# The last down projection of a two-layer FNet/GLU kernel as seven products, with weight combinations made on chip

## The chip, the cores and the metric

The kernel runs on one core of a Trainium2 chip. A core has five engines with a queue of their own each: TensorE (PE, with its weight loads shown apart as PEld), VectorE (DVE), ScalarE (ACT), GpSimd (POOL) and SyncE (SP), which here only issues DMA transfers. Each engine takes its instructions strictly in order and waits where one needs the result of another engine. The metric is the time of one execution in device microseconds; the median of three runs is given.

## The reference

Two layers of the same form; `x` is 2048 x 640, and `B_w_gate` and `B_w_up` are 640 x 1728, `B_w_down` 1728 x 640.

```python
def _A_ref(x, dft_seq_re, dft_seq_im, dft_hid_re, dft_hid_im):
    a = jnp.einsum("bsd,ed->bse", x, dft_hid_re)
    b = jnp.einsum("bsd,ed->bse", x, dft_hid_im)
    return jnp.einsum("ts,bse->bte", dft_seq_re, a) - jnp.einsum("ts,bse->bte", dft_seq_im, b)

def _B_ref(x, w_gate, w_up, w_down):
    g = jnp.einsum("bsd,df->bsf", x, w_gate)
    u = jnp.einsum("bsd,df->bsf", x, w_up)
    return jnp.einsum("bsf,fd->bsd", _sigmoid(g) * u, w_down)

for layer in range(2):
    x = x + _A_ref(_layernorm(x), ...)
    x = x + _B_ref(_layernorm(x), ...)
```

All data are float32. The kernel gets float32 accuracy from float16 matmuls: each operand is split in a high and a low part (high = cast on ACT, low = the rest, made on DVE), and a product is three matmuls, high x high, high x low and low x high (`PASSES`).

## The kernel before

`x` stays on chip as 16 tiles of 128 rows (`X`). The Fourier sublayer uses the symmetries of the matrices, so it tests on the way that the matrices given have them: `test_rows`, `test_cols`, `test_hidden_rows` and `test_hidden_cols` load pieces into two spare rooms by DMA, DVE folds them, ACT squares and sums (`square_rest`, L1337), and `test_all` reduces everything to one flag at the end. If the flag were set, a second, general program would run. Maxima of the weights (`test_w`, `test_gu`, L232) belong to these tests.

The GLU sublayer goes by four blocks of 512 rows (`b` = 0 to 3; the prediction calls layer 2's blocks 1 to 4). Each block has a gate/up stage and a down stage.

**Gate/up.** The hidden width 1728 is 13 tiles of 128 (`j` = 0 to 12) and one tile of 64 (`j` = 13). Most blocks compute two tiles per step by `seven`: gate and up of two half blocks of rows form a 2 x 2 scheme which takes seven products in place of eight (`part_one` to `part_seven`, matmuls at L1151, 128 x 256). A product is added up in a PSUM bank, copied out in between by ACT (`snap`, L1155), and DVE joins the copies (L1187, L1188). In the step behind, ACT takes the sigmoid (`gate`, L1197), DVE multiplies (`up`, L1207 and L1209), and `up_parts` splits the result into high and low (L1218 on ACT, L1219 on DVE) as the tile `ht` of the hidden activations. A step of two tiles is 108 matmuls (the first 90).

**Down.** For each of four row tiles `i`, 13 x 3 + 2 matmuls for each of two halves of the 640 columns (L1304, 128 x 320; the 64-row tile needs two). Then DVE adds the bank to `X` (L1319), and in layer 2 the row tile is stored (`store_x`). Tiles of the mirrored rows (`GB`, `GC`; `i` = 1 and 2) are stored by an indirect DMA of POOL (L381), the others by SP (L385).

**Order.** `steps` is the list of PE's stages. `at(u, f)` puts a job beside step `u`; a block of gate/up has 14 step numbers and the down behind it 8 (two for each row tile), so a step number of the third down is `block[3] - 8` to `block[3] - 1`. In `seven`, `some(n)` emits the jobs of the n-th quarter of a step between the products. Whatever is emitted earlier stands earlier in its engine's queue.

**Places.** On-chip memory is cut into units of 512 B per partition. 170 of them (units 218 to 387) are handed out by `Slots.take`, mostly to the place that has been free longest; a load into a place waits for the last reader of what lay there. For each tile of gate/up, `load_s` brings the high and low parts of the gate weight (`G`, 5 units), the four sums (`S`, 8 units) and the up weight (`U`, 3 units, or 5 for the maxima) back from DRAM, on SP. In layer 2's last block all of `U` comes in, because `test_gu` takes the maxima of `G` and `U` there. Fixed places hold `X` (80 units), two transposed inputs `XW` (34 each, by turns) and the split down weights (70).

Lines of the profile that the prediction's steps touch: `row_stats` L418, `pair_apply` L501, `pair_parts` L519 and L520, `pair_transpose` L526 (DMA transposes of the next block's input), `load_s` L1068 to L1074, `split` L239 and L241, `test_cols` L1376 to L1379 (and `test_rows` L1359 to L1362), `load_hidden_rows` L1413, `load_hidden_cols` L1422, `test_hidden_cols` L1426 and L1427.

Of the kernel before, what the change touches and what calls it, by code (L numbers as in the profile page):

```python
# [16 lines left out]
P = 128  # L17
# [32 lines left out]
DS = 2.0**11  # L50
# [4 lines left out]
PH = 2.0**-16  # L55
# [13 lines left out]
NT = 17  # L69
XTU = NT * 2  # L70
# [4 lines left out]
class Slots:  # L75
# [5 lines left out]
    def __init__(self, big):  # L81
        self.big = big
        self.live = {}
        self.freed = {}
        self.clock = 0
        self.close = False

    def take(self, n, high):
        taken = sorted(self.live.values())
        if self.close:  # L90
# [9 lines left out]
            else:  # L100
                a = min((a for f in free for a in {f[0], f[1] - n}),
# [17 lines left out]
    def new(self, a, n):  # L119
        s = Slot(self.big[:, a * UNIT : (a + n) * UNIT], (a, a + n))  # L120
        self.live[id(s)] = s.span
        return s
# [78 lines left out]
def folded(ctx, tc, pool, dram, big, acc, flag, x, ct, wh, wg, wu, wc, wd, out):  # L201
# [66 lines left out]
    def take(n, *key, high=False):  # L268
        key = key if len(key) > 1 else key[0]
        assert key not in held, key  # L270
        held[key] = slots.take(n, high)
# [105 lines left out]
    def store_x(i, g, c):  # L377
# [10 lines left out]
        for p, n in ((1, 15), (16, P - 16)):  # L388
            nc.sync.dma_start(by_twos(out, s + 2 * p, n, c), v[p : p + n])

# [141 lines left out]
    def first_combine(i):  # L532
# [11 lines left out]
    def first_parts(i):  # L544
# [6 lines left out]
    def first_transpose(i):  # L551
# [171 lines left out]
    def spill(i):  # L723

        for key in "eo":
            keep(take_parts(key, i)[:, :, :, :EC], key, i)
            drop(key, i)

# [338 lines left out]
    def load_s(j, whole=False):  # L1067
        nc.sync.dma_start(take(5, "G", j).f16, kept["w", 0, j])  # L1068
        if ("S", j) not in held:
            nc.sync.dma_start(take(8, "S", j).f16, kept["s", j])  # L1070
        if whole:
            nc.sync.dma_start(take(5, "U", j).f16, kept["w", 1, j])
            return
        nc.sync.dma_start(take(3, "U", j).f16.rearrange("p (q c) -> p q c", q=2),  # L1074
                          kept["w", 1, j].rearrange("p (q c) -> p q c", q=2)[:, :, 256:])
# [50 lines left out]
    def gated_parts(j):  # L1126
# [30 lines left out]
    def part_one(b, j):  # L1157
# [3 lines left out]
        v, w = (take(4, n, j, high=6).f32 for n in ("hv", "hw"))  # L1161
# [41 lines left out]
    def up(j):  # L1203
# [7 lines left out]
        drop("U", j)  # L1211

    def up_parts(j):
        if j not in late:
            return
        late.remove(j)
        v, s = held["hv", j].f32, take(4, "ht", j, high=True)
# [4 lines left out]
    def seven(b, j):  # L1222
# [20 lines left out]
        def mm(some):  # L1243
            ps, k = bank() if last else (None, None)
            for i in js:
                part_one(b, i)
# [15 lines left out]
            up_parts(earlier[0])  # L1262
# [7 lines left out]
            up_parts(earlier[1])  # L1270
# [4 lines left out]
            for i in js:  # L1275
                part_three(b, i)
            if last:
# [3 lines left out]
                up_parts(j)  # L1281
# [3 lines left out]
    def gate_tail(s, ps):  # L1285
# [6 lines left out]
        drop("hf", NF)  # L1292

    def down(b, i, j0, j1, store, es=(0, 1)):
# [18 lines left out]
        def post():  # L1313
# [7 lines left out]
            if store:  # L1321
                store_x(b, i, slice(es[0] * EH, (es[-1] + 1) * EH))
# [559 lines left out]
```

## Time and profile before

| | us |
|---|---|
| median of three runs | 1155.17 |
| lowest and highest | 1154.68, 1155.48 |
| the profiled execution | 1155.22 |
| its span, first to last instruction | 1153.3 |
| layer 2: down 1, gate/up 2 | 44.5, 82.7 |
| down 2, gate/up 3 | 44.5, 80.6 |
| down 3, gate/up 4 | 44.5, 80.8 |
| down 4, from there to the end | 44.6, 6.4 |

The span is that of the profiled execution, and the 1.9 us between its two numbers lie around it. A row of a group of instructions gives the line, engine, operation and tile shapes, then the busy time of the group in us and the mean of one in ns, then the time that the engine stood idle before them and what ended it. Of matmuls the mean is longer than the distance from one to the next, since they overlap: the pace is busy time by count. In a row of the timeline the first number is the start in the span, the second the length. A row of the waits gives the total, the times and the longest. The DMA share is the mean busy share of the core's 16 DMA engines.

### The profile page before, as it was taken

Reading aid. Unit: us, or ns where it says so; the run is one execution under the profiler, and the core shown is the slowest. Engines: PE = TensorE matmul, PEld = TensorE weight load, DVE = VectorE, ACT = ScalarE, POOL = GpSimd, SP = SyncE. Lnnn points to the kernel's source line nnn. Section 1 sums busy time; section 2 is a strip of 40 time slices with the busy share of each in tenths; the row PEclk is TensorE's granted clock in tenths of the full one; section 3 lists DMA queues with packets and bytes.
Section 4 is the critical chain, followed back from the end, with each engine's and each line's share of the span. In section 5 each row is a group of like instructions: output and inputs, shape, how many; then the busy total and the mean of one; then the engine's idle time right before and its main releaser. Section 6 shows DMA issues by size and latency. Waiting matters only on the chain.

```text
span 1153.3 us, 23284 instructions
## 1 busy us (share of the span) xinstructions
PE 1121.5 (97%) x9000; PEld 880.4 (76%) x9000; DVE 750.8 (65%) x1673; ACT 522.4 (45%) x1132; POOL 362.1 (31%) x581
## 2 busy tenths in 40 slices
PE   6699999999999999999999999999999999999997
PEld 2467446788878887888776888778887888788875
DVE  7996878668747676576547667726874457526740
ACT  6864485255525653365424446314551455225420
POOL 2312645232545454421530035022363112221000
PEclk9999999999999999999999999999999999999999
DMA  8418676985495949888412386566659851897401
GB/s 275 141 45 258 222 272 204 267 265 186 153 274 165 252 159 220 243 233 263 142 56 90 95 235 215 125 219 212 195 165 242 298 171 66 177 254 205 143 19 38
DMA packets 160758, 215.04 MB, mean 186 GB/s; under 512 B 74690, under 2 KB 107355, under 8 KB 160638
## 3 DMA queue, kind: packets, MB, share of 16 engines
q1 hardware_dynamic: 142078, 165.53, 48.5%
q0 software_dynamic: 18560, 47.93, 13.7%
q8 instruction: 72, 1.18, 0.4%
q14 instruction: 48, 0.39, 0.1%
HBM read 172.99 MB, written 25.81 MB: 172 GB/s over the span
## 4 chain that ended last, share of the span: by engine, by line
PE 82%; DVE 3%; DMA 2%; issue 1%; ACT 1%; SPq 0%; POOL 0%; DVEq 0%; ACTq 0%
PE acc L1151 41%; PE acc L1304 31%; PE acc L1104 4%; PE acc L899 2%; PE acc L1240 2%; PE acc L817 1%; DMA big<-in_ct 1%; DVE big L241 1%; DMA kept_w<-big 0%; DMA big<-in_wu 0%; DVE big L1188 0%; PE acc L1235 0%; SPq L257 0%; ACT big L1337 0%; DVE big L971 0%
## 5 line engine op out<-in xcount | busy, mean ns | idle before, releaser
L1151 PE MATMUL acc<-big 128*128 128x256 f16 x4698 | 516.5, 273 | 1.9 <-ACT big L1155 1.9
L1151 PEld LDWEIGHTS <-big 128*128 128x128 f16 x4698 | 459.7, 98 | 56.4 <-issue 2.3
L1304 PE MATMUL acc<-big 128*128 128x320 f16 x2624 | 357.7, 299 | 0.0
L1304 PEld LDWEIGHTS <-big 128*128 128x128 f16 x2624 | 256.8, 98 | 99.4
L1353 POOL DMA_DIRECT2D big<-in_ct x256 | 174.7, 688 | 220.4 <-DVE big L1362 122.0
L1155 ACT ACTIVATE big<-acc 128x256 f32<-128x256 f32 x348 | 129.5, 381 | 250.7 <-PE acc L1151 249.5
L1219 DVE TENSOR_TENSOR big<-big 128x512 f16<-128x512 f32 x87 | 60.0, 689 | 107.3 <-ACT big L1218 107.3
L1337 ACT ACTIVATE big<-big 128x768 f32<-128x768 f32 (+8 forms) x104 | 79.5, 764 | 106.6 <-DVE big L1362 65.0
L1104 PE MATMUL acc<-big 128*128 128x256 f16 (+1 forms) x705 | 114.9, 325 | 0.6 <-DVE big L241 0.4
L1104 PEld LDWEIGHTS <-big 128*128 128x128 f16 x705 | 68.5, 98 | 46.0 <-DVE big L241 2.0
L1319 DVE SCALAR_TENSOR_TENSOR big<-acc,big 128x320 f32<-128x320 f32 x64 | 28.5, 485 | 102.4 <-PE acc L1304 102.4
L1197 ACT ACTIVATE big<-big 128x512 f32<-128x512 f32 x87 | 53.5, 627 | 43.6 <-DVE big L1188 43.0
L241 DVE SCALAR_TENSOR_TENSOR big<-big 128x640 f16<-128x640 f32 (+6 forms) x81 | 62.4, 805 | 12.1 <-ACT big L239 12.1
L1370 POOL DMA_DIRECT2D big<-in_ct x40 | 27.4, 686 | 114.6 <-ACT big L1337 66.7
L1207 DVE SCALAR_TENSOR_TENSOR big<-acc,big 128x256 f32<-128x256 f32 x87 | 36.4, 418 | 38.7 <-PE acc L1151 33.5
L1188 DVE TENSOR_TENSOR big<-big,acc 128x512 f32<-128x512 f32 x87 | 59.2, 681 | 3.5 <-PE acc L1151 3.3
L239 ACT ACTIVATE big<-big 128x640 f16<-128x640 f32 (+7 forms) x81 | 50.5, 666 | 23.6 <-POOL big L1044 12.9
L1218 ACT ACTIVATE big<-big 128x512 f16<-128x512 f32 x87 | 54.4, 625 | 8.6 <-DVE big L1209 7.7
L899 PE MATMUL acc<-big 128*128 128x321 f16 (+3 forms) x324 | 49.0, 300 | 1.1 <-DVE big L241 1.1
L1187 DVE TENSOR_TENSOR big<-big 128x256 f32<-128x256 f32 x87 | 36.4, 418 | 14.2 <-ACT big L1155 14.1
L519 ACT ACTIVATE big<-big 128x384 f16<-128x384 f32 (+2 forms) x48 | 28.9, 648 | 35.9 <-DVE big L501 14.9
L899 PEld LDWEIGHTS <-big 128*128 128x128 f16 (+3 forms) x324 | 28.2, 95 | 20.3 <-issue 7.7
(194 smaller groups left out, 1033.2 us busy)
## 6 DMA issues: line engine op xcount, KB each, us to landing
big<-kept_s SPq DMA_DIRECT2D x84, 512.0 KB
big<-kept_w SPq DMA_DIRECT2D x115, 320.0 KB
big<-in_ct POOLq DMA_DIRECT2D x256, 128.0 KB, 4.0
big<-kept_w SPq DMA_DIRECT2D x74, 192.0 KB
kept_w<-big SPq DMA_DIRECT2D x27, 320.0 KB
big<-in_ct POOLq DMA_DIRECT2D x32, 256.0 KB, 5.1
kept_s<-big SPq DMA_DIRECT2D x13, 512.0 KB
big<-in_wg SPq DMA_DIRECT2D x18, 320.0 KB
```

Of the source, the lines that this page charges most:

```text
L241: nc.vector.scalar_tensor_tensor(dl, src, s, dh, op0=OP.mult, op1=OP.subtract)
L899: nc.tensor.matmul(ps[:m, :EC], z[:, at : at + m], w[:, 384 * wp : 384 * wp + EC], start=(d == 0 and zp == HI and wp == HI), stop=(d == ND ...
L1104: nc.tensor.matmul(ps, w[wp][:, d * P : (d + 1) * P], xt[:, xp, :], start=(d == 0 and wp == HI and xp == HI), stop=(d == ND - 1 and wp == LO))
L1151: nc.tensor.matmul(ps, wt, xt, start=start and n == 0, stop=n == len(todo) - 1, skip_group_check=not start)
L1155: nc.scalar.activation(dst, ps, AF.Copy)
L1188: nc.vector.tensor_tensor(v, v, other, op=OP.add)
L1197: nc.scalar.activation(v, v, AF.Sigmoid, scale=SG)
L1218: nc.scalar.activation(s.parts[HI], v, AF.Copy)
L1219: nc.vector.tensor_tensor(s.parts[LO], v, s.parts[HI], op=OP.subtract)
L1304: nc.tensor.matmul(held["pd", e][0][:, :EH], held["ht", j].parts[hp][:, i * P : (i + 1) * P], held["w", 2, j].parts[wp][:, e * EH : (e + 1 ...
L1337: nc.scalar.activation(v, v, AF.Square, accum_out=new_sum()[:p])
L1353: nc.gpsimd.dma_start(v[:, g], bass.AP(ct.tensor, (r * S + row) * S, [[P, NS], [d * S, 16], [1, P]]))
```

## The change

In layer 2's last block (`PAIRED = (), (3,)`) the down is made of pairs of hidden tiles, `NP = 6` pairs for `j` = 0 to 11: rows of the block in two halves, a pair's two tiles, and the two column halves form a 2 x 2 times 2 x 2 product, which takes seven products. Tiles 12 and 13 are added in the plain way.

- `up_parts` calls `first_parts` and `second_parts`, and `sum_parts` follows at the end of the step: they make, split and keep three of the four quarters (`A`, 6 units a pair) and four sums of them (`AS`, 8 units a pair).
- The right sides' combinations are made in the third down: `load_raw` (POOL) loads raw weight tiles, `make_t` forms four differences in place on DVE, `split_t` splits them into `TT`, which lies over `X`'s tiles 0 to 7 and over the `XW` that is free then.
- `down_pairs` runs the seven products, adds them up in four banks for each of two row tiles, and adds to `X` also in the middle of a sum.
- Stores of row tiles of the first three blocks are put beside the gate/up behind (`store_later`).
- `test_gu` goes to layer 2's third block, with the whole `U` loaded there, and the last block loads the part of `U`. In it `G` and `U` share a place of 8 units, and the three loads are put at different times.
- Tests of hidden rows and columns are put later and closer together; hidden columns are loaded by POOL. In layer 1 one row (`fw`) is kept in DRAM for a while. The sums that end the Fourier sublayer for the third block (`combine`, `join_hidden`, `add_hidden` with `q` = 2) are put 3.2 steps earlier in both layers, so that two of them lie in the first gate/up and not in the first down; the load of a block's second tile is put 1.3 steps later.
- `DS` and `PH`, powers of two, change from 2^11 and 2^-16 to 2^9 and 2^-18.

```diff
+NP = 6
+PAIRED = (), (3,)
...
-    def take(self, n, high):
+    def take(self, n, high, top=0):
         taken = sorted(self.live.values())
+        if top:
+            free = [a for a in [top - n * (i + 1) for i in range(NP)] + list(range(UNITS - n, FIX - 1, -2))
+                    if all(a + n <= c or d <= a for c, d in taken)]
+            assert free, f"no room for {n}: {taken}"
+            return self.new(free[0], n)
+        if self.fours and not high:
+
+            m = -n % 4 + n
+            free = [a for a in range(-FIX % 4 + FIX, UNITS - m + 1, 4) if all(a + m <= c or d <= a for c, d in taken)]
+            assert free, f"no room for {n}: {taken}"
+            low = [a for a in free if a + m <= self.limit]
+            a = min(low, key=lambda a: max(self.freed.get(u, 0) for u in range(a, a + m))) if low and n < 15 else free[0]
+            return self.new(a, n, m)
...
+    def store_later(b, g, c):
+
+        if b < NB - 1:
+            at(block[b + 1] + 2.2 + 1.2 * g + c.start / D, store_x, b, g, c)
+        else:
+            store_x(b, g, c)
...
+        if "G" in do:
+            v = take(8, "GU", j).f32
+            held["G", j], held["U", j] = Slot(v[:, : 5 * UNIT], None), Slot(v[:, 5 * UNIT :], None)
+            nc.sync.dma_start(held["G", j].f16, kept["w", 0, j])
+        if "S" in do and ("S", j) not in held:
+            nc.sync.dma_start(take(8, "S", j).f16, kept["s", j])
+        if "U" in do:
+            nc.sync.dma_start(held["U", j].f16.rearrange("p (q c) -> p q c", q=2),
+                              kept["w", 1, j].rearrange("p (q c) -> p q c", q=2)[:, :, 256:])
...
+    def first_parts(p, v):
+        a = both(take(6, "A", p, top=UNITS - 8 * NP), 768)[:, :, :256]
+        f = take(8, "af", p).f32
+        nc.vector.tensor_tensor(f[:, 512:768], v[:, :256], v[:, 256:], op=OP.subtract)
+        nc.scalar.activation(a[:, 0], v[:, :256], AF.Copy)
+        nc.vector.tensor_tensor(a[:, 1], v[:, :256], a[:, 0], op=OP.subtract)
+
+    def second_parts(p, v, w):
+        a, f = both(held["A", p], 768)[:, :, 256:], held["af", p].f32
+        s1, s2, s4 = (f[:, 256 * n : 256 * (n + 1)] for n in (0, 1, 3))
+        nc.scalar.activation(a[:, 0], w, AF.Copy)
+        nc.vector.tensor_tensor(s1, v[:, 256:], w[:, 256:], op=OP.add)
+        nc.vector.tensor_tensor(s2, s1, v[:, :256], op=OP.subtract)
+        nc.vector.tensor_tensor(s4, w[:, :256], s2, op=OP.subtract)
+        nc.vector.tensor_tensor(a[:, 1], w, a[:, 0], op=OP.subtract)
+
+    def sum_parts(p):
+        f, s = held["af", p].f32, both(take(8, "AS", p, top=UNITS), 1024)
+        for c in (slice(0, 512), slice(512, 1024)):
+            nc.scalar.activation(s[:, 0, c], f[:, c], AF.Copy)
+        for c in (slice(0, 512), slice(512, 1024)):
+            nc.vector.tensor_tensor(s[:, 1, c], f[:, c], s[:, 0, c], op=OP.subtract)
+        drop("af", p)
...
+    def load_raw(p):
+        for k in range(2):
+            j = 2 * p + k
+            v = take(5, "dr", j) if p % 2 else fixed(XU + XTU + 20 + 5 * k, 5, "dr", j)
+            nc.gpsimd.dma_start(v.f32, wd[j * P : (j + 1) * P, :])
+
+    def make_t(p):
+
+        v, w = (held["dr", 2 * p + k].f32 for k in range(2))
+        b11, b12, b21, b22 = v[:, :EH], v[:, EH:], w[:, :EH], w[:, EH:]
+        nc.vector.tensor_tensor(b11, b12, b11, op=OP.subtract)
+        nc.vector.tensor_tensor(b12, b22, b12, op=OP.subtract)
+        nc.vector.tensor_tensor(b22, b22, b11, op=OP.subtract)
+        nc.vector.tensor_tensor(b21, b21, b22, op=OP.subtract)
+
+    def split_t(j, do):
+        split(*TT[j].parts, held["dr", j].f32, DS, do)
...
+    CHAIN = {1: "a", 2: "c", 5: "b", 3: "b", 4: "d", 6: "a", 7: "a", 8: "a"}
+    READ = {1: (0, 0), 2: (0, 0), 5: (1, 1), 3: (0, 1), 4: (1, 0), 6: (0, 1), 7: (1, 0), 8: (1, 1)}
+    REST = (2, 3, 4, 8)
...
+                for p in range(NP) if n < 8 else ():
...
+                    mms += [(a[:, ap], w[:, wp]) for ap, wps in PASSES for wp in wps]
+                r, e = READ[n]
+                c = (i + 2 * r) * P
+                for j in range(2 * NP, NF + 1) if n in REST else ():
+                    mms += [(held["ht", j].parts[hp][:, c : c + P], held["w", 2, j].parts[wp][:, e * EH : (e + 1) * EH])
+                            for hp, wps in (PASSES if j < NF else PASSES[:1]) for wp in wps]
...
-        nc.sync.dma_start(room(3 * r + j)[:n, :D], wh[r, j * P : j * P + n, :])
+        nc.gpsimd.dma_start(room(3 * r + j)[:n, :D], wh[r, j * P : j * P + n, :])
...
+                if first or b < last:
+                    order = [[(n, 0), (n, 1)] for n in (1, 5, 2, 3, 6, 4, 7, 8)]
+                else:
+                    order = [[(n, 0), (n, 1)] for n in (1, 5)] + [[(m, i), (n, i)] for i in range(2) for m, n in ((6, 2), (7, 3), (4, 8))]
+                steps += [down_pairs(b, todo, not first) for todo in order]
+                for p in range(NP):
+                    u = block[b] - 7.7 + 1.25 * p
+                    at(u - (0.3 if p == 0 else 1.0), load_raw, p)
+                    at(u + 0.3, make_t, p)
+                    for v in range(2):
+                        for k in range(2):
+                            at(u + 0.4 + 0.1 * v, split_t, 2 * p + k, (v,))
...
-                            at(block[last] + j // 2 * 2 + 0.6, test_gu, j)
+                            at(block[2] + j // 2 * 2 + 0.6, test_gu, j)
```

`order` is the list of products and row tiles of the last down: 1 and 5 for both row tiles, then for each row tile 6 and 2, 7 and 3, 4 and 8. After each, `post` adds the bank to `X`; once both contributions of a row tile's half are in, it is stored (direct rows by halves, indirect rows whole).

185 lines of the change are left out of this document (149 added, 36 removed).

## Prediction

> **What bounds the kernel now.** I read the share of each engine first, then who TensorE (PE) waited for, then the chain that ended last.
>
> ```profile
> PE 1121.5 (97%) x9000; PEld 880.4 (76%) x9000; DVE 750.8 (65%) x1673; ACT 522.4 (45%) x1132; POOL 362.1 (31%) x581
> ```
> ```profile
> PE twin L353 <- ACT big L359: 12.3, 6, 7.9
> ...
> PE acc L1151 <- ACT big L1155: 1.9, 1, 1.9
> ```
> ```profile
> 1021.55 71.40 PE acc L1151 x654
> ...
> 1102.26 44.57 PE acc L1304 x328
> 1146.85 0.49 DVE big L1319
> ```
>
> PE is busy for 97%. Its long waits lie in the opening (the "twin" lines); in the gate/ups in seven products (L1151) it waits once, 1.9 us, and in the downs (L1304) never. The chain is PE to the last down (328 matmuls, 44.57 us), one eviction, and then a tail. So a matmul taken out of the last down comes off the time at the pace of that stage, if PE is still never kept waiting. The table by stage says what the other engines have left; I number layer 2's four blocks 1 to 4, each a gate/up and a down.
>
> ```profile
> 428.70:473.20 44.50, 44.50 (x330) 32.07 (x329) 25.44 (x62) 13.88 (x26) 18.39 (x27) 1.00 1.02 251
> ...
> 769.20:851.90 82.70, 80.77 (x741) 72.23 (x739) 59.39 (x137) 41.37 (x97) 30.99 (x54) 1.00 0.59 193
> ...
> 896.40:977.00 80.60, 80.60 (x741) 72.22 (x739) 45.63 (x111) 40.31 (x93) 15.77 (x32) 1.00 0.50 173
> 977.00:1021.50 44.50, 44.50 (x330) 32.07 (x329) 21.00 (x41) 10.64 (x20) 13.10 (x11) 1.00 0.87 207
> 1021.50:1102.30 80.80, 80.80 (x741) 72.27 (x739) 51.42 (x96) 39.43 (x101) 8.08 (x7) 1.00 0.60 180
> 1102.30:1146.90 44.60, 44.52 (x328) 31.84 (x326) 9.79 (x33) 3.08 (x6) 2.95 (x4) 1.00 0.07 28
> 1146.90:1153.30 6.40, 0.00 (x0) 0.00 (x0) 0.44 (x1) 0.00 (x0) 0.00 (x0) 0.85 0.10 33
> ```
>
> Columns: the stretch and its length, busy time of PE, PEld, DVE, ACT, POOL, PE's clock, DMA share, GB/s. Gate/up 2 (769 to 852) is the one that runs 2 us long. The clock is full in every stage.
>
> **What the matmuls give.** Before, the last down runs 4 row tiles x 2 halves x 41 (13 x 3 + 2) = 328. After, seven products x 2 row tiles x 6 pairs x 3 passes = 252; tiles 12 and 13 (3 + 2 passes) stay plain for four outputs x 2 row tiles, 40. Total 292: 36 fewer. The pace is 44.57 / 328 = 0.136 us, so 36 x 0.136 = **4.9 us off**.
>
> ```profile
> L1304 PE MATMUL acc<-big 128*128 128x320 f16 x2624 | 357.7, 299 | 0.0
> L1304 PEld LDWEIGHTS <-big 128*128 128x128 f16 x2624 | 256.8, 98 | 99.4
> ```
>
> The group agrees: 357.7 / 2624 = 0.136. Weight loads take 0.098 each and fit under it. The Trainium skill (TensorE: Matmul & The Clock Gate, Back-to-back issue gap) gives columns / 2.4 + 2.5 ns for an isolated gap, 135.8 ns here, but for a stream of load-and-multiply pairs 131 ns at 512 columns and 81 at 128; between these, 320 columns would go at some 106 ns (an estimate) and 36 be worth 3.8 us. This trace shows such a stream at 136, so the row is used.
>
> **What is added in the last gate/up and down.**
>
> ```profile
> L1155 ACT ACTIVATE big<-acc 128x256 f32<-128x256 f32 x348 | 129.5, 381 | 250.7 <-PE acc L1151 249.5
> L1219 DVE TENSOR_TENSOR big<-big 128x512 f16<-128x512 f32 x87 | 60.0, 689 | 107.3 <-ACT big L1218 107.3
> L1218 ACT ACTIVATE big<-big 128x512 f16<-128x512 f32 x87 | 54.4, 625 | 8.6 <-DVE big L1209 7.7
> L241 DVE SCALAR_TENSOR_TENSOR big<-big 128x640 f16<-128x640 f32 x41 | 37.4, 935 | 3.3 <-ACT big L239 3.3
> L1187 DVE TENSOR_TENSOR big<-big 128x256 f32<-128x256 f32 x87 | 36.4, 418 | 14.2 <-ACT big L1155 14.1
> L239 ACT ACTIVATE big<-big 128x640 f16<-128x640 f32 x41 | 28.9, 726 | 0.0
> ```
> ```profile
> L232 DVE TENSOR_REDUCE wmax<-big 128x1 f32<-128x640 f16 x18 | 13.5, 809 | 0.0
> ...
> L1427 DVE TENSOR_TENSOR big<-big 128x319 f32<-128x319 f32 x4 | 2.0, 491 | 0.1
> L1319 DVE SCALAR_TENSOR_TENSOR big<-acc,big 128x320 f32<-128x320 f32 x2 | 0.9, 487 | 5.8 <-PE acc L1304 5.8
> ```
>
> DVE in gate/up 4: a pair of hidden tiles costs two casts' rests now, 2 x 0.689. Paired it costs five 256-wide and three 512-wide operations, 5 x 0.418 + 3 x 0.689 = 4.16, so 2.78 more a pair and 16.7 in all. Eighteen maxima (L232) leave, 13.5, three tests of hidden rows (a 512-wide difference each) and one of hidden columns come in from the downs beside it, some 3 us. 51.4 - 13.5 + 16.7 + 3 = 58 of 80.8 us, as much as gate/up 2 has. ACT gets one 256-wide and three 512-wide casts a pair for two: 0.38 + 3 x 0.625 - 1.25 = 1.0, six pairs 6 us, to 45. The new sums are cast behind the step's products, and their rests run on DVE in the first 4 us of the next step, where DVE has no product to wait for. I cost both at nothing for PE. In down 4 sixteen evictions of 0.49 (8 more) lie under 39.7 us of matmuls. The tightest reuse of a bank is product 6 to product 7: DVE must have read the one before PE adds the other, and 23 matmuls, 3.1 us, lie between for one eviction.
>
> **What is added in the third down.** Twelve raw tiles (320 KB) are loaded by POOL, 24 half-row differences are made on DVE and 12 tiles split on ACT and DVE. No row shows a 128x320 difference from SBUF; 128x319 takes 0.49 and the 128x320 eviction 0.49, so 24 x 0.49 = 11.8; the rests 12 x 0.935 = 11.2; three hidden-row tests leave, 3 x 0.69 = 2.1. DVE: 21.0 + 11.8 + 11.2 - 2.1 = 41.9, and some 0.8 us of waiting for ACT's cast (0.726) at each pair, 4.8 more: 46.7. If casts overlap wholly it is 41.9; if every raw tile also came 2 us late, 71. I take 46.7, beside 44.5 of PE.
>
> ```profile
> 1028.88 0.43 DVE L1187 TENSOR_TENSOR big<-big 128x256 f32<-128x256 f32 x1 [5.23 <-ACT big L1155]
> ```
> ```profile
> 997.44 6.05 SPq L526 DMA_TRANSPOSE big<-big  x2
> ```
>
> The overrun is hidden: the next operation of DVE that gate/up 4 needs starts at 1028.9, 7.4 us behind the down's end. The nearer limit is the transposed input of gate/up 4: its last transposes are issued by 1003.5 and needed at 1021.5, 18 us. They are queued on SP behind DVE's parts, and DVE now has two pairs' differences and one or two pairs' rests before them (8 x 0.49 + 4 x 0.935 = 7.7). That fits too. DMA: 12 x 0.328 MB at 251 / 1.02 = 246 GB/s is 16 us of all engines; three loads of hidden rows (100 rows x 1024 f32 each, 1.2 MB, 5) and four stores (1.3 MB, 5.3) leave: 0.87 x 44.5 + 16 - 10.3 = 44.4 of 44.5. That is full; the row at 428.7 shows such a down, at a share of 1.02, with PE busy throughout.
>
> ```profile
> 982.85 1.13 DVE L501 TENSOR_SCALAR big<-big,small 128x640 f32<-128x640 f32 x2
> ...
> 989.47 2.14 DVE L501 TENSOR_SCALAR big<-big,small 128x640 f32<-128x640 f32 x2
> ```
> ```profile
> 989.01 2.31 POOL L1413 DMA_DIRECT2D big<-in_wh  x2 [6.51 <-ACT big L1337]
> ```
>
> The same two operations took 1.13 and 2.14 us. The Trainium skill (SBUF — State Buffer, Who interferes with whom) has a DVE operation in a two-port mode and a GpSimd one shut each other out, and two POOL loads lie beside the second pair. With raw loads on POOL beside both pairs, DVE's sum would by that rule be 1.0 larger, 47.7.
>
> **What is moved.** Eighteen maxima go to gate/up 3: 45.6 + 13.5 = 59 of 80.6 us on DVE, and 128 KB more for each of nine loads. Stores of the first three blocks go from the downs into the gate/up behind them, on SP and POOL; SP no longer stands in the down until an indirect store lands. Hidden columns go from SP to POOL, which has 8 us of work in gate/up 4. The first layer's one spilled row and the earlier sums (q = 2) are a few operations under PE, behind the last weights that block 1 waits for. But places are handed out by age, so all these shift which place a later load waits for. The only trace of what that costs is gate/up 2:
>
> ```profile
> 829.05 0.43 DVE L1360 TENSOR_TENSOR big<-big 128x256 f32<-128x256 f32 x1 [1.56 <-DMA big<-in_ct]
> ...
> 833.51 0.68 DVE L1188 TENSOR_TENSOR big<-big,acc 128x512 f32<-128x512 f32 x1
> ...
> 834.22 0.63 ACT L1197 ACTIVATE big<-big 128x512 f32<-128x512 f32 x1 [0.30 <-DVE big L1188]
> ...
> 835.59 0.64 ACT L1155 ACTIVATE big<-acc 128x256 f32<-128x256 f32 x2
> ...
> 836.00 6.17 PE L1151 MATMUL acc<-big 128*128 128x256 f16 x55 [1.93 <-ACT big L1155]
> ```
>
> DVE stood for test data, came late to the sums of the step before (L1188), the sigmoid (L1197) came late behind them and the copy of a product (L1155) behind that. PE's step began about 826.2 (72 matmuls of 0.109 and the stall before 836.0), so DVE may come some 6 us late into a step; beyond, PE waits. I keep this stall at 1.9; its ends are 0 (the test data come earlier) and 3.8 (a second one like it).
>
> **The tail.**
>
> ```profile
> 1135.58 0.89 DVE L1319 SCALAR_TENSOR_TENSOR big<-acc,big 128x320 f32<-128x320 f32 x2 [10.25 <-PE acc L1304]
> ...
> 1146.85 0.49 DVE L1319 SCALAR_TENSOR_TENSOR big<-acc,big 128x320 f32<-128x320 f32 x1 [5.08 <-PE acc L1304]
> ```
> ```profile
> 1136.74 0.96 POOL L381 DMA_INDIRECT out<-big,rows  x1 [9.91 <-DVE big L1319]
> ```
> ```profile
> DMA to landing us min/median/max: 3.0/5.4/7.9
> ```
> ```profile
> SPq L385 <- DMA out<-big,rows: 44.1, 3, 25.1
> ```
>
> The last indirect store starts 0.3 us behind its eviction, and direct stores wait on SP until it has landed. After, it follows product 3 of the second row tile, 28 matmuls (3.8 us) before the end: issued at -3.8 + 0.5 + 0.3 = -3.0 from PE's end, landed at 0.0 with the shortest landing. The last direct store comes at +0.5 as before. I take the shortest, as nothing else moves then, so 0 for the tail; with the median, +2.2 (landing at 2.4, some 0.3 to issue the first of two stores, against 0.5), with the longest +4.7.
>
> **Sum.** 1155.22 (the profiled execution; span 1153.3 and 1.9 around it) - 4.9 = **1150.3**. The median of the runs, 1155.17, is 0.05 lower, which changes nothing.
>
> **Rivals.** *The last indirect store ends it*, landing at its median: 1150.3 + 2.2 = 1152.5, at the most 1155.0. For: the wait rows. Against: the queue is empty then. 0.10. *The maxima in gate/up 3 stall PE*: DVE then has 59 of 80.6 us there, as in gate/up 2, which stalled, and four maxima (3 us) come in one go in each step. It decides where DVE comes over 6 us late. Against: gate/up 4 had these same maxima and did not stall. One or two stalls of 1.9: 1152.2 to 1154.1. 0.15. *Banks are handed over late in down 4*: ten reuses that each wait out an eviction (0.49 and some 0.1) give 6 back: 1156. Against: 3.1 us lie between the tightest two. 0.05. *The saving is that of weight loads*, 36 x 0.098 = 3.5: 1151.7; against, PEld is busy 32 of 44.5 us. 0.03. (The skill's section on the issue gap, above, would give 1155.2 - 3.8 = 1151.4.) *Slower: gate/up 4 runs out of places.* Of 170 units the new left sides take up to 84, so loads of sums can be issued only as the step before frees their place.
>
> ```profile
> 814.29 0.32 SPq L1070 DMA_DIRECT2D big<-kept_s  x1
> ```
>
> Here one was issued as late as its step began (about 814.4), was needed 39 matmuls of 0.109, 4.3 us, on, and PE did not wait. If two such loads (1 MB, 4.3 us at 246 GB/s) stand behind the stores and tests in each of five steps, they come 6 to 7 us late into the step and cost 2 to 2.5 a step: 1150.3 + 11 = 1161. It decides from a landing later than 4.3 us. 0.12, with lesser cases near 1155.
>
> **The numbers.** Forecast 0.55, from 1148.4 (the 1.9 stall gone) to 1152.2 (once more). With the tail's and the maxima's rivals that is 0.80: 1148.4 to 1155.0. About 0.2%, 2.3 us, is what a measurement of this kernel can tell from no change. Faster than 1152.9: the forecast, weight loads, half of the tail and of the maxima, 0.70. Within: the rest of these, the banks and the milder late loads, 0.18. Slower: 0.12.
>
> **What would show it.** Down 4 with 292 matmuls in 39.7 us; no wait of PE on DVE there; gate/up 3 and 4 at 80.6 to 80.8; DVE near 42 busy in the third down; 6.4 us from PE's end to the span's. A gate/up longer than 81, or a tail beyond 7, makes it wrong.

## The result and the profile after

The kernel after takes 1183.14 us (median of 4 runs, 1179.4 to 1186.73) against 1154.95 of the kernel before on the same chip: 1.024 times as long, 95% interval 1.0221 to 1.0258. Forecast was 1150.3. The profiled execution took 1183.73, its span is 1181.9, 28.6 longer than before.

First PE's share and its waits, from the page and the table of waits (total, times, longest):

```profile
PE 1124.5 (95%) x8964; PEld 879.7 (74%) x8964; DVE 787.9 (67%) x1753; ACT 535.3 (45%) x1156; POOL 376.2 (32%) x599
```
```profile
PE acc L1209 <- DMA big<-big: 11.6, 2, 7.1
...
PE acc L1209 <- ACT big L1213: 9.3, 6, 7.3
...
PE acc L1209 <- DMA big<-kept_s: 3.0, 1, 3.0
PE acc L1209 <- DMA big<-kept_w: 3.0, 1, 3.0
```

L1209 is the seven products' line (L1151 before), L1213 the copy of a product (L1155). PE, which waited once in these stages, now waits 3 us or more in four places (and five more times for under 0.6 us each). The timeline of PE says where (in brackets the idle time ahead and what ended it):

```profile
226.81 72.58 PE L1209 MATMUL acc<-big 128*128 128x256 f16 x648 [3.00 <-DMA big<-kept_w]
...
389.94 44.16 PE L1209 MATMUL acc<-big 128*128 128x256 f16 x384 [7.27 <-ACT big L1213]
...
1042.45 0.40 PE L1209 MATMUL acc<-big 128*128 128x256 f16 x1 [7.06 <-DMA big<-big]
1047.39 29.30 PE L1209 MATMUL acc<-big 128*128 128x256 f16 x242 [4.55 <-DMA big<-big]
...
1092.10 28.67 PE L1209 MATMUL acc<-big 128*128 128x256 f16 x261 [3.01 <-DMA big<-kept_s]
```

Two stalls lie in layer 1, which the new down doesn't touch; two are the start of gate/up 4, on DMA from SBUF to SBUF, the transposes of its input; one lies inside gate/up 4. They sum to 24.9 us. The matmuls behind three of them are slow: an undisturbed gate/up makes 654 in 71.40, 0.1092 each; here 648 take 72.58, 384 take 44.16 and 242 take 29.30, 1.8 + 2.2 + 2.9 = 6.9 more. The third down, gate/up 4 in two pieces, the tail and gate/up 3, by windows (stretch and length, PE, PEld, DVE, ACT, POOL, clock, DMA share, GB/s), and the chain's last row:

```profile
990.60:1035.40 44.80, 44.78 (x331) 32.06 (x328) 36.48 (x70) 16.56 (x27) 11.43 (x16) 1.00 0.78 155
1035.40:1127.00 91.60, 76.41 (x668) 66.49 (x669) 50.19 (x106) 40.79 (x108) 19.58 (x20) 0.93 0.78 203
1127.00:1135.40 8.40, 7.90 (x73) 6.93 (x72) 7.41 (x17) 4.68 (x12) 0.00 (x0) 1.00 0.01 2
...
1175.20:1181.90 6.70, 0.00 (x0) 0.00 (x0) 0.48 (x1) 0.00 (x0) 0.00 (x0) 0.81 0.17 57
910.00:990.60 80.60, 80.60 (x740) 72.22 (x739) 58.32 (x129) 40.29 (x93) 17.60 (x35) 1.00 0.63 214
```
```profile
1135.49 39.68 PE acc L1469 x292
```

The last down does what was forecast: 292 matmuls in 39.68, 4.9 less. Gate/up 3 with the maxima is 80.60 as before. The tail is 6.7 (6.4 before). Stalls 24.9, slower matmuls 6.9, tail 0.3, less 4.9, make 27.2 of the 28.6; 1.1 of the rest are short waits in gate/up 4.

**The start of gate/up 4.** SP's queue, before (first fence; its second pair of transposes, 6.05 us, stands in the prediction) and after. A row's length is the time that SP's queue stood on the two transposes; they land later:

```profile
987.91 8.80 SPq L526 DMA_TRANSPOSE big<-big  x2
```
```profile
1006.11 9.05 SPq L551 DMA_TRANSPOSE big<-big  x2
...
1017.92 24.08 SPq L551 DMA_TRANSPOSE big<-big  x2
```

The downs start at 976.8 and 990.7, so the second pair is issued 6.6 us later in the down, and holds the queue for 24 us where it was 6. The queue is through with it at 1042.0, and PE's second wait for it ends at 1047.39, when its last part has landed; PE needed it at 1035.4. ACT's timeline, ahead of the second pair, shows why it is later, and POOL's loads show why it is slower:

```profile
1015.00 0.74 ACT L257 ACTIVATE big<-big 128x640 f16<-128x640 f32 x1 [0.32 <-DVE big L1419]
1015.64 0.83 ACT L544 ACTIVATE big<-big 128x768 f16<-128x768 f32 x1
```
```profile
1022.74 0.54 POOL L1410 DMA_DIRECT2D big<-in_wd  x1 [11.96 <-DVE big L259]
1023.63 1.60 POOL L1410 DMA_DIRECT2D big<-in_wd  x3 [0.35 <-DVE big L259]
1025.22 4.71 POOL L1624 DMA_DIRECT2D big<-in_wh  x4
```

The cast of the input's last part (L544) stands on ACT behind the split of a combination (L257), which waited for the differences (L1419). And raw weights (L1410) and hidden rows (L1624) are loaded while the transposes run.

### The profile page after: what moved, and what is told of

It reads as the page before. It is cut to its first block, busy times and chain, and to the rows that moved or that the text cites. A ratio compares the mean times of both kernels' runs of the same rounds, so it can differ in the third digit from the quotient of the medians.

```text
span 1181.9 us, 23419 instructions
## 1 busy us (share of the span) xinstructions
PE 1124.5 (95%) x8964; PEld 879.7 (74%) x8964; DVE 787.9 (67%) x1753; ACT 535.3 (45%) x1156; POOL 376.2 (32%) x599
## 4 chain that ended last, share of the span: by engine, by line
PE 63%; DMA 11%; DVE 7%; issue 4%; ACT 2%; POOL 1%; SPq 0%; DVEq 0%; ACTq 0%; POOLq 0%
PE acc L1209 36%; PE acc L1515 15%; PE acc L1469 3%; PE acc L1153 3%; DMA big<-big 3%; DMA big<-in_ct 3%; PE acc L934 2%; PE acc L1308 2%; DMA big<-kept_w 2%; DVE big L259 1%; DMA big<-kept_s 1%; PE acc L852 1%; DMA big<-in_wd 1%; DMA big<-in_wh 1%; DVE big L545 1%
## 5 line engine op out<-in xcount | busy, mean ns | idle before, releaser
L1209 PE MATMUL acc<-big 128*128 128x256 f16 x4698 | 524.3, 275 | 27.0 <-DMA big<-big 11.6
L1209 PEld LDWEIGHTS <-big 128*128 128x128 f16 x4698 | 462.5, 99 | 86.6 <-issue 14.6
L1515 PE MATMUL acc<-big 128*128 128x320 f16 x2296 | 313.0, 299 | 0.0
L1515 PEld LDWEIGHTS <-big 128*128 128x128 f16 x2296 | 224.7, 98 | 87.0
L1213 ACT ACTIVATE big<-acc 128x256 f32<-128x256 f32 x348 | 127.8, 381 | 230.0 <-PE acc L1209 227.8
L1153 PEld LDWEIGHTS <-big 128*128 128x128 f16 x705 | 68.5, 98 | 46.0 <-DVE big L259 2.1
L1287 DVE TENSOR_TENSOR big<-big 128x512 f16<-128x512 f32 x75 | 51.6, 689 | 75.7 <-ACT big L1286 75.7
L259 DVE SCALAR_TENSOR_TENSOR big<-big 128x640 f16<-128x640 f32 (+6 forms) x93 | 72.4, 810 | 13.5 <-ACT big L257 13.2
L257 ACT ACTIVATE big<-big 128x640 f16<-128x640 f32 (+7 forms) x93 | 59.4, 675 | 47.3 <-DVE big L1417 19.3
L1530 DVE SCALAR_TENSOR_TENSOR big<-acc,big 128x320 f32<-128x320 f32 x56 | 24.8, 484 | 58.4 <-PE acc L1515 58.3
L1246 DVE TENSOR_TENSOR big<-big,acc 128x512 f32<-128x512 f32 x87 | 59.2, 681 | 3.5 <-PE acc L1209 3.3
L1286 ACT ACTIVATE big<-big 128x512 f16<-128x512 f32 x75 | 47.0, 627 | 13.4 <-DVE big L1267 12.0
L1245 DVE TENSOR_TENSOR big<-big 128x256 f32<-128x256 f32 x87 | 36.4, 418 | 23.5 <-ACT big L1213 23.3
L1570 DVE TENSOR_TENSOR big<-big 128x256 f32<-128x256 f32 x64 | 26.4, 413 | 37.4 <-DMA big<-in_ct 37.4
```

What stands on the lines that cost most here:

```text
L257: nc.scalar.activation(dh, src, AF.Copy, scale=s)
L259: nc.vector.scalar_tensor_tensor(dl, src, s, dh, op0=OP.mult, op1=OP.subtract)
L1153: nc.tensor.matmul(ps, w[wp][:, d * P : (d + 1) * P], xt[:, xp, :], start=(d == 0 and wp == HI and xp == HI), stop=(d == ND - 1 and wp == LO))
L1209: nc.tensor.matmul(ps, wt, xt, start=start and n == 0, stop=n == len(todo) - 1, skip_group_check=not start)
L1213: nc.scalar.activation(dst, ps, AF.Copy)
L1246: nc.vector.tensor_tensor(v, v, other, op=OP.add)
```

## The experiments

Theory A: layer 1's stalls come of the earlier sums of `q` = 2, whose places shift the places of all later loads. Its rival B: they come of the later load of the second tile. Theory C: the stall at gate/up 4's start is the combinations' own, by DVE's order (C1) or by traffic beside the transposes (C2). Its rival: the stores and loads that were moved make the transposes late. Theory D: gate/up 4's late loads come of DVE standing for test rows, so that places come free late. Its rival: they come late by their own order, or because the DMA is full there.

| run | median, us | ratio to before, 95% |
|---|---|---|
| after | 1183.14 | 1.0221 to 1.0258 |
| after, q = 2 back (e1) | 1172.45 | 1.0113 to 1.0165 |
| after, no combinations (e4) | 1163.54 | 1.0039 to 1.0087 |
| before, q = 2 earlier (e3) | 1158.70 | 1.0019 to 1.0040 |
| before, load later (e6) | 1157.71 | 0.9999 to 1.0031 |
| before, both (e7) | 1171.42 | 1.0066 to 1.0152 |
| e1, no raw loads (e12) | 1158.81 | 1.0010 to 1.0036 |
| e1, raw loads alone (e13) | 1156.58 | 0.9998 to 1.0031 |
| e1, combinations later (e8) | 1162.10 | 1.0026 to 1.0070 |
| e8, layer 1's load back (e14) | 1160.43 | 1.0023 to 1.0057 |
| e14, tests spread (e17) | 1158.52 | 1.0011 to 1.0037 |
| e14, third block's stores back (e18) | 1157.92 | 1.0009 to 1.0037 |
| e14, both (e19) | 1155.38 | 0.9995 to 1.0029 |
| e19, tests behind loads (e20) | 1155.29 | 0.9985 to 1.0008 |
| before, tests behind loads (e21) | 1155.58 | 0.9994 to 1.0012 |

**Layer 1 (e1, e3, e6, e7).** In the kernel after, the sums were put back (e1); in the kernel before, the sums (e3), the second tile's load (e6) and both (e7) were moved. Each of these edits acts in both layers, e7 too, whose expectation names layer 1 alone:

```diff
-(block[0] + 11.4, block[1] + 3.5)[q - 2] + n
+(block[0] + 14.6, block[1] + 3.5)[q - 2] + n
```
```diff
-(8, 7.9, 4.5, 3.5))[j], load_s, j
+(8, 6.6, 4.5, 3.5))[j], load_s, j
```

> The changed kernel, but the sums of the third block (q = 2) stand at their old step in both layers. Theory A: the two stalls of the first layer (3.0 us at 224 and 7.3 us at 383, and some 4 us at a lower clock behind them) come from these sums, whose places shift the places of all later loads; then about 1169 us, with the first layer as before. Rival B: they come from the earlier-load edit (second tile of a block, 1.3 steps later); then about 1183 us, as the changed kernel.

> The kernel before with one edit of the change: the sums of the third block (q = 2) 3.2 steps earlier. Theory A: some 14 us slower than before (1169 us), with stalls in the first layer. Rival B: 1155 us.

> The kernel before with one edit of the change: the second tile of a block is loaded 1.3 steps later. Rival B: some 14 us slower (1169 us). Theory A: 1155 us.

e1 is 10.7 faster than after, and both stalls of layer 1 are gone from its profile. But e3 costs the kernel before 3.6 only: the stall near 224 is there, that near 383 isn't. Its time is neither theory A's (1169) nor rival B's (1155): theory A was half of it. e6 costs 2.6, with an interval that touches no change, and shows neither stall. So both edits at once:

> The kernel before, with two edits of the change in layer 1: the sums of q = 2 3.2 steps earlier, and the second tile's load 1.3 steps later. Theory A2 (these two together make both stalls of layer 1, and neither alone does): stalls of 2 to 3 us near 224 and of 4 to 7.3 us near 383 with slower matmuls behind each, 1163 to 1168. Rival (the two only add up: 3.6 and 2.6 over before): no stall near 383, 1158 to 1161; then a third edit of layer 1, the spilled row or the moved stores, is needed for the second stall.

1171.42, 16.3 over before (single runs from 1162.7 to 1173.4), and both stalls as in the kernel after. The profiled execution is 18.1 over before: 14.2 of that lie in layer 1, and 4.0 in gate/up 2, where PE's waits sum to 4.1 and were 1.9. PE's timeline of e7 in layer 1:

```profile
226.39 72.58 PE L1151 MATMUL acc<-big 128*128 128x256 f16 x648 [2.72 <-DMA big<-kept_w]
...
388.84 44.87 PE L1151 MATMUL acc<-big 128*128 128x256 f16 x384 [6.68 <-ACT big L1155]
```

Two edits that cost 3.6 and 2.6 alone cost 16.3 together. SP's queue shows how. Before, then e6, then e7, then after:

```profile
203.95 6.89 SPq L526 DMA_TRANSPOSE big<-big  x2
...
313.11 13.97 SPq L526 DMA_TRANSPOSE big<-big  x4
```
```profile
315.73 6.72 SPq L526 DMA_TRANSPOSE big<-big  x2
...
324.25 11.71 SPq L526 DMA_TRANSPOSE big<-big  x2
```
```profile
317.73 6.67 SPq L526 DMA_TRANSPOSE big<-big  x2
...
326.19 12.61 SPq L526 DMA_TRANSPOSE big<-big  x2
```
```profile
208.57 6.18 SPq L551 DMA_TRANSPOSE big<-big  x2
...
318.16 6.65 SPq L551 DMA_TRANSPOSE big<-big  x2
...
326.61 15.26 SPq L551 DMA_TRANSPOSE big<-big  x2
```

The earlier sums make a pair of transposes 4.6 us late (208.57 for 203.95), and the loads that stand on SP behind it: the 3.0 us on `kept_w` near 224. The later load comes to stand between two pairs, so its transfer runs beside the second pair: from the first to the last transpose it was 14.0 us, and is 20.2 in e6, 21.1 in e7 and 23.7 in after. The queue is through with the last transpose at 327.1 before and at 336.0 in e6, 2.6 of that by an earlier delay of that run, but at 338.8 in e7 and 341.9 in after. Wherever the load is moved, eight test loads then come on POOL in one go: in e1 (first fence) 17.9 us into the gate/up, in after (second fence) 20.8. In after DVE stands 9.3 us for them:

```profile
366.00 5.53 POOL L1564 DMA_DIRECT2D big<-in_ct  x8 [0.92 <-issue]
```
```profile
373.79 5.53 POOL L1564 DMA_DIRECT2D big<-in_ct  x8 [0.92 <-issue]
```
```profile
380.03 0.43 DVE L1570 TENSOR_TENSOR big<-big 128x256 f32<-128x256 f32 x1 [5.93 <-DMA big<-in_ct]
383.78 0.43 DVE L1571 TENSOR_TENSOR big<-big 128x256 f32<-128x256 f32 x1 [3.33 <-DMA big<-in_ct]
...
386.51 0.68 DVE L1246 TENSOR_TENSOR big<-big,acc 128x512 f32<-128x512 f32 x1
```

Behind it the joins (L1246), the sigmoid, the copy, and PE: the same chain as the prediction showed for gate/up 2, but 7.27 us and not 1.9. Over all profiles with the load moved, DVE's two waits for these test data and PE's stall behind them grow together: 1.9 us and no stall in e6, 2.7 and none in e1, 4.1 and 1.2 in e13, 5.4 and 2.5 in e12, 7.2 and 4.9 in e8, 9.3 and 7.3 in after, 9.4 and 6.7 in e7. e8, e12 and e13 have the sums at their old step. So the later load can make this stall without the sums, and the two together make it longest; how the late transposes delay the test loads is not shown.

**The combinations (e4, e12, e13, e8).** e4 takes out the raw loads, differences and splits; the products read stored weight tiles, so the combinations are missing from the result.

```diff
-                    at(u - (0.3 if p == 0 else 1.0), load_raw, p)
-                    at(u + 0.3, make_t, p)
...
-        return both(TT[2 * p + (n in (2, 4))], EH, int(n in (2, 3)))
+        return both(held["w", 2, 2 * p + (n in (2, 4))], EH, int(n in (2, 3)))
```

> The changed kernel without the weights' combinations: the twelve raw loads, the differences and their splits are left out, and the seven products read stored weight tiles in their place, so that the output differs. Theory C: the 11.6 us stall ahead of the last gate/up and some 3 us at a lower clock behind it come from this work in the third down, which delays the DMA transposes; then about 1168 us, with a third down and last gate/up of 125.3 us together, as before. Rival D: the transposes are late because of the stores and loads that were moved; then about 1183 us.

1163.54, 19.6 less than after; the stall at gate/up 4's start is gone. The next two, on e1, split this cost. e12 keeps DVE's and ACT's work without the traffic; e13 keeps the loads, with one 256-wide difference a pair and no split:

```diff
-            nc.gpsimd.dma_start(v.f32, wd[j * P : (j + 1) * P, :])
+            nc.gpsimd.memset(v.f32, 0.0)
```
```diff
-        nc.vector.tensor_tensor(b11, b12, b11, op=OP.subtract)
...
+        nc.vector.tensor_tensor(v[:, :256], v[:, 256:512], w[:, :256], op=OP.subtract)
```

> The kernel after, with the sums of q = 2 back, and the twelve raw weight tiles filled with zeros on POOL instead of being loaded: the differences and splits on DVE and ACT stay, 3.9 MB of DMA leave (so the combinations are left out of the result). Theory C2 (the traffic beside them makes the second pair of transposes take 24 us): they take 6 to 9 us, still issued near 1018, the stall falls from 12.6 to under 3 us, 1157 to 1162. Rival (DVE's order makes the stall, the traffic little): transposes still at 15 us or more or their issue late, stall over 7 us, 1166 to 1172.

> The kernel after, with the sums of q = 2 back, and the raw tiles loaded at the same steps, but only one difference of 256 columns made of each pair and no split; the products read the stored weight tiles in place of the combinations, which are left out. Some 21 of 23 us of DVE's work leave the third down, the traffic stays. Theory C2 (traffic): the second pair of transposes is issued some 7 us earlier than 1018 and still takes over 12 us; the stall keeps half or more of its 12.6 us unless the earlier issue makes up for it, 1160 to 1168. Rival (DVE's order): the stall goes, 1155 to 1159.

The second pair of transposes in e1, e12 and e13:

```profile
1004.80 25.24 SPq L551 DMA_TRANSPOSE big<-big  x2
```
```profile
1008.82 5.17 SPq L551 DMA_TRANSPOSE big<-big  x2
```
```profile
1000.72 17.42 SPq L551 DMA_TRANSPOSE big<-big  x2
```

e12: without the traffic 5.17 us, late but short, and 13.6 us are back. e13: still 17.42 beside the traffic, but it begins early enough: the queue is through at 1018.1, PE comes to gate/up 4 at 1023.4 and doesn't wait for it, and 15.9 are back. So neither C1 nor C2 alone: each half of the cost fits into the slack of 18 us, and the two together don't. e8 keeps all the work and begins it 2.5 steps later, behind the input's parts:

```diff
-                    u = block[b] - 7.7 + 1.25 * p
+                    u = block[b] - 5.2 + 1.2 * p
```

> The kernel after, with the sums of q = 2 back at their old step, and the weights' combinations begun 2.5 steps later (their loads too), so that the transposed input of gate/up 4 goes first. Against 1172.45 with the sums alone put back. Theory C1 (the stall is that the combinations stand in front of the input's parts on DVE and their loads beside its transposes): the second pair of transposes takes 6 to 9 us and is issued by 1012, the 12.6 us stall goes, 1153 to 1158. Rival (DVE is too full from the third down to the middle of gate/up 4 wherever the work stands): the stall moves into gate/up 4 as waits on DVE's or ACT's work, 1164 to 1170.

1162.10, 10.4 less than e1, and nothing is left of the stall at gate/up 4's start. The expected 1158 was missed: the profiled execution (1166.33, the slowest of five) has one stall of 4.87 near 385 in layer 1, and two on late loads in gate/up 4, 4.8 together. Its transposes tell more about the traffic: 12.67 us beside four raw tiles alone (hidden rows are loaded behind them), against 5.17 with none (e12) and 17 to 25 beside more raw tiles and hidden rows (e13, e1).

**What is left (e14, e17 to e21).** e14 puts the second tile's load of layer 1 back as well, `7.9 if first else 6.6`.

> The kernel after, with the combinations 2.5 steps later, and both edits of layer 1 back (sums of q = 2, and the second tile's load at its old step in layer 1 alone). Theory A2 (the two edits together hold up layer 1): no stall near 383 (4.9 us in the run with the load's edit kept), and of the rest only the late loads of gate/up 4, some 5 us with slower matmuls behind: 1154 to 1158 against 1162.1. Rival (the load's edit alone does nothing, as 1157.7 against 1155.1 in the kernel before says): the stall near 383 stays in some executions, 1159 to 1164.

1160.43: no stall of layer 1 in the profile, but only 1.7 faster, which is not clear of noise, and above the range. In gate/up 4 PE still waits 4.5 us for loads, and DVE stands there 4.9 us for test rows; theory D takes the second for the cause of the first. e17 spreads the tests; e18 puts the third block's stores back into the third down; e19 does both:

```diff
-21.5 + 0.9 * (4 * r + k), 1.5)
+21.5 + 1.2 * (4 * r + k), 2.0)
...
-29.6 + 0.7 * (3 * r + j), 1.2)
+31.6 + 0.8 * (3 * r + j), 1.3)
```
```diff
-        if b < NB - 1:
+        if b < NB - 2:
             at(block[b + 1] + 2.2 + 1.2 * g + c.start / D, store_x, b, g, c)
```

> The kernel with three edits (1160.43), and in gate/up 4 the tests of the hidden matrices spread over more steps: rows 1.2 steps apart and each test 2.0 behind its load (were 0.9 and 1.5), columns 0.8 and 1.3 (were 0.7 and 1.2). Theory D (in gate/up 4 DVE stands for test rows, so the second parts come late, places come free late, and the sums' loads of the next step land late): the waits of PE on those loads fall from 4.5 to under 2 us, 1152 to 1156. Rival (the places come free too late by the order of the loads themselves, or the DMA is full there whatever waits on it): still 3 to 5 us, within 1.5 us of the kernel with three edits.

> The kernel with three edits, and the stores of the third block back in the third down, where they were before the change (1.3 MB, 5.3 us of all DMA engines, leave gate/up 4). Theory D2 (the traffic of gate/up 4 makes its loads late): waits of PE on loads there fall by 2 us or more, 1155 to 1158. Rival (the third down was the fuller place, so its transposes or the first loads of gate/up 4 come late): 1161 to 1166.

> Both edits together, on the kernel with three. If both theories hold, waits of PE on loads in gate/up 4 under 1 us: 1150.5 to 1154, the kernel before less some of the 4.9 us of the last down. If neither does, 1159 to 1164.

Alone they give 1.9 and 2.5, which is not clear of noise, and leave 3.7 and 3.5 us of waits: e18's time lies where expected, e17's above its range, and neither takes 2 us of the waits away. In gate/up 4 DVE stands for no test row any more in e17, and in e18 for 7.8 us while PE waits less than in e14, so theory D by itself is not the cause. Together they give 5.1, just clear of noise, to 1155.38 (above the 1154 expected), and the waits on loads in gate/up 4 sum to 1.2 us. That tests and traffic each hold up the loads, and either is enough, fits this and is not shown further. In e19 the transposes of both pairs are short, as most raw tiles are loaded behind them, and the windows of gate/up 3 to down 4 stand thus:

```profile
989.38 7.13 SPq L551 DMA_TRANSPOSE big<-big  x2
...
999.53 6.35 SPq L551 DMA_TRANSPOSE big<-big  x2
```
```profile
897.90:978.50 80.60, 80.60 (x741) 72.23 (x739) 58.48 (x129) 40.30 (x93) 18.01 (x35) 1.00 0.62 212
978.50:1023.00 44.50, 44.50 (x330) 32.07 (x329) 32.20 (x62) 15.10 (x24) 12.07 (x17) 1.00 0.77 221
1023.00:1105.90 82.90, 81.23 (x740) 71.95 (x738) 58.54 (x123) 46.24 (x117) 18.70 (x20) 1.00 0.72 188
1105.90:1145.60 39.70, 39.70 (x293) 28.38 (x290) 16.23 (x45) 4.79 (x10) 2.95 (x4) 1.00 0.09 31
```

Of the 4.9 us, this run (span 1152.5) loses 2.1 in gate/up 4 (82.9 for 80.8), some 1 in gate/up 2, whose stall is 2.92 here, and 0.5 in the tail. Two earlier kernels with the spread tests (e15, e16) ran 4249 and 4246 us and say nothing on the theories: as I read them, a test's square is taken after the next load has taken its room, the flag is set, and the general program runs.

e20 and e21 go at gate/up 2's stall: in layer 2 the tests of rows and columns stand 1.4 of their pace behind their load, in e19 and in the kernel before.

```diff
-                at(u + pace, test, *key)
+                at(u + (1 if first else 1.4) * pace, test, *key)
```

> The kernel with three edits, both edits of gate/up 4 (tests spread, stores back), and in layer 2 each test of the first three gate/ups 1.4 of its pace behind its load, no longer 1.0 (its square 1.9, no longer 1.7). If the stall of gate/up 2 (2.9 us in the run without this edit, 1.9 in the kernel before) comes of DVE standing for test data, it goes: 1150.5 to 1153.5 against 1155.4, below the kernel before. If it comes of DVE's amount of work there, nothing changes: 1154.5 to 1157.

> The kernel before with that last edit alone. If the stall of gate/up 2 comes of standing for test data: 1152.8 to 1153.8, 1.9 us less. If of the amount of work: 1155 to 1156.

Nothing: 1155.29 and 1155.58. In e21 the 1.93 became 0.90 and 0.94 at two places, in e20 2.17 and 0.84. The edit shortens DVE's waits for test data and doesn't end them: in e21 one of 1.10 is left of 1.42 and 1.56, in e20 two of 1.14 and 1.09. In e21 PE's stalls sum to 1.84 with 1.9 us less of waiting on DVE, which speaks against test data; that it is the amount of DVE's work is the rival that is left, not shown. No version measurably below the kernel before came of it.

## Why the prediction was wrong

**The last down: right.** 292 matmuls at 0.136, 39.68 us, no wait on DVE. The rival that only weight loads are saved (0.03) is out.

**DVE in the last gate/up and the third down: right in size.** Gate/up 4 has 57.6 us of DVE's work (50.19 and 7.41 in its two windows; 58 forecast), e19 58.5. The third down has 36.5 (41.9 forecast): 2.1 us of the last pair are done behind it, and the rests of the splits took 0.82 each, not 0.935. The two operations that took 1.13 and 2.14 before took 1.13 both times, the second beside four raw loads of POOL, so the 1.0 us that the prediction held possible for DVE beside POOL loads did not come here. The overrun itself delays nothing: e12 keeps this work and has no stall at gate/up 4's start.

**The step that failed first** is "The nearer limit is the transposed input of gate/up 4" with its 18 us and "That fits too", with "That is full; the row at 428.7 shows such a down, at a share of 1.02, with PE busy throughout." The 7.7 us of DVE in front were near (the pair is issued 6.6 later). But the transposes were kept at 6 us; beside raw weights and hidden rows they held the queue for 24 (25 in e1). 7 + 18 us more is beyond the slack. The 18 us were also counted from the end of the queue's row, and the last part landed 5.4 us behind that (1047.39 for 1042.0). A share of 1.02 had been read as harmless because PE was busy beside it. But in that down the four transposes began 9.6 us into it and were through 18.7 us ahead of its end (438.28 to 454.50), so the row couldn't show what becomes of a pair issued late. The sum of 44.4 in 44.5 was off as well: the share over the third down was 0.78, and above 1 only where the transposes run. This cost 11.6 of waits and 2.9 of slower matmuls; leaving the combinations out gives 19.6 back, some 4 of it in smaller stalls elsewhere (2.2 and 5.1 in layer 1, 2.0 in gate/up 4).

**The second** is in "What is moved": the earlier sums and the later load were costed at nothing but a shift of gate/up 2's stall (0 to 3.8). The sums were called "a few operations under PE"; what had to be costed is that they push a pair of transposes 4.6 us back, and SP's loads behind it 3.7 to 3.9. The load's move was named in the change, and the sum priced it at nothing at all. Together they cost 16.3 in the kernel before, most of it in layer 1. Their chain, DVE late on test data, was shown in the prediction at 1.9 us, so the mechanism was known and its place and size were not. No rival held layer 1.

**The slower rival** (gate/up 4 runs out of places, 11 us, 0.12) was right in kind: loads of sums come late, 3.0 us in after and 4.5 to 4.8 in e8 and e14, against 11. The tests and stores moved there, taken together, made up most of it (e19); neither did alone.

**The maxima in gate/up 3** (0.15) cost nothing: 80.60 us with 58.3 of DVE, 59 forecast. **The tail**: 6.7 against 6.4; the indirect store lands early enough, so the rival at 1152.5 is out. **Banks**: no wait.

**The price of a stall** lacked a term: behind 3.0, 7.3 and 11.6 us of idle PE the matmuls ran at half clock for a while, 1.8, 2.2 and 2.9 us more. Behind the 3.01 us near 1089 they didn't.

What stays open: the 2.1 us of gate/up 4 in e19, and why its runs spread from 1152.9 to 1162.3 where the kernel before has 1154.6 to 1158.3. Some of the spread arises in the opening: in the profiles of e6 and e8 the granted clock is 0.51 and 0.52 from 50 to 60, where before has 1.00, and all that follows is some 2.6 us later.

## What to carry to other kernels

Slack is one account for all who draw on it: price a moved transfer or a new batch of work by what the queue behind it will do when everything else that is moved has drawn as well, and test the edits in pairs, since two that cost 3 us each may cost 16. Where a DMA transpose feeds the next stage, give it an empty window: put no load between its pairs, and begin new loads and new work on DVE and ACT behind it. A change that saves 4.9 us in one place is worth only what its preparation leaves, so place the preparation first.

## What the runs showed of the hardware

DMA transposes stretch with what runs beside them: a pair held SP's queue for 5.17 us with neither raw tiles nor hidden rows (e12), 11.0 and 12.7 beside four raw tiles (e14, e8), and 17 to 25 beside more raw tiles and hidden rows (e13, after, e1), though the loads were issued by POOL and the transposes by SP. The windows of the kernel after within its second pair:

```profile
1015.00:1020.00 5.00, 5.00 (x39) 3.61 (x37) 3.50 (x6) 1.47 (x2) 0.00 (x0) 1.00 1.27 154
...
1025.00:1030.00 5.00, 5.00 (x39) 3.60 (x37) 3.10 (x6) 1.47 (x2) 4.94 (x5) 1.00 1.08 357
1030.00:1035.00 5.00, 5.00 (x39) 3.60 (x38) 4.58 (x9) 1.47 (x2) 0.00 (x0) 1.00 1.19 154
```

At a share above 1 the traffic was 357 GB/s in the window in which POOL issued loads throughout, and 154 in the two others: here the share, not GB/s, told whether there was room. The Trainium skill (DMA: Bandwidth & Descriptors, Issuing engines are not separate DMA queues) says that transfers issued by different engines run on the same 16 DMA engines and interleave; these traces agree, with the lengths above.

The clock of PE falls in a stall. After, from 1034 on:

```profile
1036.00:1038.00 2.00, 0.00 (x0) 0.00 (x0) 1.93 (x4) 0.74 (x1) 0.00 (x0) 1.00 0.92 110
1038.00:1040.00 2.00, 0.00 (x0) 0.00 (x0) 1.23 (x3) 0.00 (x0) 0.48 (x1) 0.84 1.46 125
1040.00:1042.50 2.50, 0.05 (x1) 0.06 (x2) 0.19 (x1) 0.00 (x0) 0.68 (x1) 0.50 1.27 122
...
1049.00:1052.00 3.00, 3.00 (x16) 2.06 (x14) 0.00 (x0) 0.47 (x2) 0.00 (x0) 0.50 0.62 228
1052.00:1055.00 3.00, 3.00 (x25) 2.48 (x23) 0.00 (x0) 0.60 (x2) 0.00 (x0) 0.83 0.00 0
```

Some 4 us after PE stopped at 1035.3 the clock is at 0.50, and it stays there for 5.6 us after PE starts again at 1047.4 (0.83 is the mean of 1 us at 0.50 and 2 at 1.00). The Trainium skill (TensorE: Matmul & The Clock Gate, Part 1: The HAM clock gate) has the clock halve after at least one idle window of about 3.4 us and come back after at least one busy one, and the windows run free of the kernel. Both lengths here are more than one window and less than two, which agrees. But a stall shorter than a window was enough near 224: behind 3.00 us of idle PE the clock was 0.50 from 227 to 229, and behind 2.21 us in e4 from 228 to 230, while behind 3.01 us near 1089 it stayed at 1.00.
